# Starting with half the queries, spreading the first keys, values and weight pieces, and moving the last gates to VectorE, in a top-k attention and two-MLP kernel

## The chip, the core and the metric

The kernel runs on one NeuronCore of a Trainium2 chip. The core has five engines with a program each, which run in their own order and wait for one another through semaphores: TensorE (PE in the rows; PEld is its weight load), VectorE (DVE), ScalarE (ACT), GpSimd (POOL) and SyncE (SP). SP issues every transfer of this kernel. The metric is the device time of one execution in microseconds (us); lower is better.

## The reference

Four batches of eight heads with 576 positions and 64 dimensions each go through an attention that keeps the 32 largest scores of each row, then through two MLPs on 2304 rows of 512 values, with 2048 hidden units and no normalisation between them.

```
scores = (q @ k^T) / 8                        # q, k, v: (4, 8, 576, 64)
kth    = 32nd largest of each row of scores
scores = where(scores >= kth, scores, -1e9)
attn   = softmax(scores);  x = attn @ v       # x: (2304, 512)
h = x @ w_in1;  x = (h * sigmoid(h)) @ w_out1 # w_in1: (512, 2048), w_out1: (2048, 512)
h = x @ w_in2;  out = elu(h) @ w_out2
```

## The kernel before

**Tiles and slots.** The 2304 rows are cut into 18 chunks of 128 rows, and a chunk has one tile per head, 144 tiles in all. The program is one loop over slots, `for s in ...: slot(s)`. In slot s, DVE does the first half of tile s's top-k and the second half of tile s-1's. A top-k is four MAX8 (eight largest, L622), three MATCH_REPLACE8 (strike them out, L626) and one masked product (L645) on 128x576 values. PE makes tile s+1's scores S (L587) and multiplies tile s-3's weights with the values (L690).

**MLP steps.** From slot 12 on most slots also hold one MLP step, four steps for a chunk and layer, 12 slots between the layers. A step's 48 matmuls h (L750) stand in slot s, its gate in s+1, its 12 matmuls a (L798) in s+2. The gate is: ACT reads h from PSUM and makes u and t (`emit_act`, L764 to L772), POOL combines them into t (`emit_g`, L778), ACT rounds t to float16 (`emit_ghi`, L782) and POOL forms the remainder (`emit_glo`, L162). The tile of u has one buffer, those of t, gh and the h banks two each. After the last tile's slot only MLP steps are left, and the last four steps, of chunk 17 in layer two, stand in slots 160 to 163.

**Between the layers.** When a chunk's first MLP is complete, `x2_copy` reads it (L811), a sum of squares gives a power-of-two scale, and ACT scales and rounds it (`x_hi`, L159 and L719); POOL forms the remainder (`x_lo`, L162) and SP issues the transposing transfer xt<-x (`x_tp`, L729) that layer two's h needs. In before this stands at the end of the slot five after the step (`p5`).

**Weights.** The four weight matrices arrive as 64-bit numbers, in 64 pieces of 512 KB (`w_load`, L258). DVE, ACT and POOL turn them into 32-bit numbers during slots -2 to 11. `PIECES` says how many pieces each of these slots takes. A piece of the first matrix costs one DVE instruction (L283), which needs one from ACT first (y, L276); a piece of the others costs two on DVE (L316, L321). Per pair of pieces there is a POOL addition (L288 or L308). Each matrix then gets a trace (L341, L346) that sets its scale, after which its pieces are rounded at points of three per slot (`w_point`, L365 to L370) or by `w_scaled` and `w_split`.

**Order.** Each engine runs its instructions in the order in which slot() writes them, and `prep(slots, ...)` puts a load, its sum of squares and its rounding into three slots. `late` lists run at a slot's end, and their second halves (`after`) early in the next slot. Every transfer from SP waits for the one eight places before it.

Of the kernel before, what the change touches and what calls it, by code (L numbers as in the profile page):

```python
# [32 lines left out]
def kernel(  # L33
# [493 lines left out]
    def q_hi(ch):  # L527
        t, m = qnat[ch], qsc[ch]
        if ch == 0:
            scaled(t, m[:, 1:2])  # L530
            a = [p.tile([128, H, 2, D], F16, tag=n, name="q16") for p, n in ((x16_p, "x16"), (u_p, "u"))]
            tb = t[:, :, None, :].to_broadcast([128, H, 2, D])
            nc.scalar.activation(out=a[0], in_=tb, func=AF.Copy)
            qnat[ch] = (tb, a)
            return
# [28 lines left out]
    def q_tp(g):  # L564
# [193 lines left out]

    def emit_act(l, ch, i):
        ps = hps.pop((l, ch, i))  # L760
        u = u_p.tile([128, 512], F32, tag="u", name="u")
        t = t_p.tile([128, 512], F32, tag="t", name="t")
        if l == 0:
            nc.scalar.activation(out=u, in_=ps, func=AF.Tanh, scale=c1[ch])  # L764
            nc.scalar.activation(out=t, in_=ps, func=AF.Copy)
            nc.scalar.activation(out=u, in_=u, func=AF.Identity, scale=G1, bias=g1)
        else:
            c = c2[ch]
            nc.scalar.activation(out=u, in_=ps, func=AF.Relu, scale=c[:, 1:2])
# [443 lines left out]
```

## Time and profile before

| | before |
|---|---|
| median of 3 runs | 1114.62 us (1113.91 to 1117.53) |
| the profiled execution | 1119.21 us, of it 1117.5 us span |
| PE busy | 995.0 us (89%) |
| DVE busy | 941.4 us (84%) |
| ACT busy | 884.2 us (79%) |
| POOL busy | 811.8 us (73%) |
| tile 0's first MAX8 starts | 17.02 us |
| tile 12's first MAX8 starts | 177.33 us |
| tile 143's masked product ends | 1018.00 us |
| last matmul ends | 1113.75 us |

The span runs from the first to the last instruction of the profiled execution. An engine's busy share is a mean over three quite different stages: the start to about 180 us, in which the weights are converted, the middle, and the end from 1018 us on, in which DVE has nearly nothing left.

### The profile page before, as it was taken

The page shows a single profiled execution, that of the slowest core. Times are in us where ns is not written, and L with a number is a line of the kernel's source. Part 1 is how long each engine was busy: PE and PEld are TensorE (multiplying, and loading weights), DVE is VectorE, ACT ScalarE, POOL GpSimd, SP SyncE. Part 2 cuts the span into 40 slices and gives each one's busy share as a digit, 9 for nine tenths or more (in the row PEclk, how much of TensorE's full clock was granted, in tenths as well). Part 3 has the DMA queues.
Part 4 walks back from the last instruction along what each step waited for, and adds up shares of the span by engine and source line. Part 5 has one row for each costly group of instructions (what it writes and reads, how often), then busy time and mean ns, then how long its engine had stood idle before and what let it go on. Part 6 is the DMA issues. An engine that isn't in the chain of part 4 may idle for free.

```text
span 1117.5 us, 30872 instructions
## 1 busy us (share of the span) xinstructions
PE 995.0 (89%) x11956; PEld 715.7 (64%) x11956; DVE 941.4 (84%) x2203; ACT 884.2 (79%) x1539; POOL 811.8 (73%) x971
## 2 busy tenths in 40 slices
PE   1265778689999999999999999999999999999997
PEld 0223336366766777777767777776677777777755
DVE  2899998999898999999998999999899999994000
ACT  6877767989887898989888898988777777776554
POOL 4787886877777777777777777877767676776643
PEclk9978889889999999999999999999999999999999
DMA  7999883555587656566676756567755545443100
GB/s 263 323 270 276 249 205 86 101 94 115 114 136 141 119 95 121 117 110 123 122 160 144 120 111 114 118 114 132 135 101 105 92 83 82 87 68 54 30 20 10
DMA packets 386034, 141.34 MB, mean 126 GB/s; under 512 B 361568, under 2 KB 368736, under 8 KB 385888
## 3 DMA queue, kind: packets, MB, share of 16 engines
q1 hardware_dynamic: 385888, 139.38, 60.6%
q8 instruction: 93, 1.52, 0.6%
q14 instruction: 53, 0.43, 0.1%
HBM read 52.17 MB, written 21.10 MB: 66 GB/s over the span
## 4 chain that ended last, share of the span: by engine, by line
PE 36%; POOL 20%; issue 10%; DVE 8%; DMA 5%; ACT 4%; SPq 0%; POOLq 0%; ACTq 0%; DVEq 0%
PE h L750 16%; PE a L798 15%; POOL t L778 5%; POOL gh L162 4%; DVE r L626 3%; DVE m L622 3%; POOL e L671 3%; DMA xt<-x 2%; PE S L587 2%; PE av L690 2%; POOL W L671 2%; DMA et<-e 2%; POOL x L162 1%; DVE e L645 1%; ACT gh L782 1%
## 5 line engine op out<-in xcount | busy, mean ns | idle before, releaser
L750 PE MATMUL h<-xt,W 128*128 128x128 f16 x6912 | 413.2, 220 | 9.2 <-DMA xt<-x 8.3
L750 PEld LDWEIGHTS <-W 128*128 128x128 f16 x6912 | 397.5, 98 | 22.9 <-DMA xt<-x 10.1
L798 PE MATMUL a<-W,gh 128*128 128x512 f16 x1728 | 397.4, 379 | 4.1 <-POOL gh L162 2.0
L622 DVE MAX8 m<-r 128x8 f32<-128x576 f32 x432 | 313.0, 750 | 2.6
L798 PEld LDWEIGHTS <-gh 128*128 128x128 f16 x1728 | 159.1, 98 | 178.1 <-POOL gh L162 5.0
L162 POOL TENSOR_TENSOR gh<-t,gh 128x512 f16<-128x512 f32 x144 | 167.1, 1160 | 69.8 <-ACT gh L782 69.8
L626 DVE MATCH_REPLACE8 r<-m,r 128x576 f32<-128x576 f32 x288 | 214.2, 744 | 0.0
L778 POOL TENSOR_TENSOR t<-u,t 128x512 f32<-128x512 f32 x144 | 183.2, 1272 | 29.9 <-ACT u L772 23.5
L782 ACT ACTIVATE gh<-t 128x512 f16<-128x512 f32 x144 | 90.2, 627 | 90.5 <-POOL t L778 89.3
L637 ACT ACTIVATE e<-S,bias,c 128x576 f32<-128x576 f32 x144 | 119.8, 832 | 43.2 <-DVE r L626 23.9
L671 POOL TENSOR_TENSOR e<-e,e 128x512 f16<-128x512 f32 x87 | 100.9, 1160 | 71.7 <-ACT e L665 69.5
L587 PE MATMUL S<-kt,qt 128*128 128x288 f16 (+1 forms) x640 | 97.4, 293 | 48.7 <-DVE sv L134 19.5
L622 DVE MAX8 m<-S 128x8 f32<-128x576 f32 x144 | 109.6, 761 | 32.7 <-PE S L587 32.4
L587 PEld LDWEIGHTS <-qt 128*128 128x128 f16 (+1 forms) x640 | 55.3, 101 | 105.4 <-issue 49.2
L645 DVE SCALAR_TENSOR_TENSOR e<-S,m,e 128x576 f32<-128x576 f32 x144 | 115.5, 802 | 0.1
L626 DVE MATCH_REPLACE8 r<-m,S 128x576 f32<-128x576 f32 x144 | 107.7, 748 | 0.0
L671 POOL TENSOR_TENSOR W<-e,W 128x512 f16<-128x512 f32 x57 | 66.2, 1161 | 44.7 <-ACT W L665 38.7
L690 PE MATMUL av<-vt,et 128*128 128x64 f16 (+1 forms) x2100 | 79.9, 195 | 9.0 <-DMA et<-e 8.8
L690 PEld LDWEIGHTS <-et 128*128 128x128 f16 (+1 forms) x2240 | 73.7, 101 | 17.2 <-DMA et<-e 10.8
L665 ACT ACTIVATE e<-e 128x576 f16<-128x576 f32 x87 | 58.8, 676 | 24.9 <-DVE e L645 9.5
L365 PE MATMUL lo<-W,eye 128*128 128x512 f32 x84 | 54.9, 741 | 20.6 <-ACT W L370 12.7
L635 ACT ACTIVATE bias<-m,fixed,c 128x1 f32<-128x1 f32 x144 | 54.1, 376 | 9.6 <-DVE m L622 9.4
(128 smaller groups left out, 1272.5 us busy)
## 6 DMA issues: line engine op xcount, KB each, us to landing
W<-in_moe_w_in_dram SPq DMA_DIRECT2D x32, 512.0 KB, 7.4
W<-in_moe_w_out_dram SPq DMA_DIRECT2D x20, 512.0 KB, 5.8
qd<-q SPq DMA_DIRECT2D x34, 256.0 KB, 5.0
kn<-in_k_dram SPq DMA_DIRECT2D x16, 288.0 KB, 3.2
qn<-in_q_dram SPq DMA_DIRECT2D x16, 256.0 KB, 3.4
out_dram<-o SPq DMA_DIRECT2D x16, 256.0 KB, 2.5
vd<-v SPq DMA_DIRECT2D x12, 320.0 KB, 2.7
vt<-vd SPq DMA_DIRECT2D x22, 160.0 KB, 2.9
```

Of the source, the lines that this page charges most:

```text
L162: nc.gpsimd.tensor_tensor(dst, x, hi, op=ALU.subtract)
L587: nc.tensor.matmul(out=ps[n * e:n * e + n, a, 0:HALF], lhsT=qt[:, 2 * (t % 2) + p, n * e:n * e + n], rhs=kT[bh][:, a * HALF:(a + 1) * HALF ...
L622: nc.vector.max(st["m8"][:, i, :], src if i == 0 else st["r"])
L626: nc.vector.match_replace(out=fold(r) if i == 0 else r, in_to_replace=st["m8"][:, i, :], in_values=src if i == 0 else r, imm_value=LOW,)
L637: nc.scalar.activation(out=fold(e), in_=src, func=AF.Exp, scale=c[:, 0:1], bias=bias)
L645: nc.vector.scalar_tensor_tensor(e, src, st["m8"][:, n - 1, 7:8], e, op0=ALU.is_ge, op1=ALU.mult, accum_out=sums[ch][:, j:j + 1])
L671: nc.gpsimd.tensor_tensor(h[:, S + LO:2 * S], e[:, 0:SF], h[:, 0:SF], op=ALU.subtract)
L690: nc.tensor.matmul(out=avs[ch][n * e:n * e + n, bh[1], :], lhsT=et[:, c, n * e:n * e + n], rhs=vT[bh][:, x, y:y + D], start=(i == 0), stop ...
L750: nc.tensor.matmul(out=ps[:, f:f + 128], lhsT=w, rhs=xt[:, z, :], start=(kk == 0 and x == 0), stop=(kk == KDM - 1 and x == 2),)
L778: nc.gpsimd.tensor_tensor(t, u, t, op=ALU.add if l else ALU.mult)
L782: nc.scalar.activation(out=gh[:, 0, :], in_=gf[l, ch, i], func=AF.Copy)
L798: nc.tensor.matmul(out=acc, lhsT=gh[:, z, u * 128:(u + 1) * 128], rhs=W[:, n, w * 512:(w + 1) * 512], start=(m == 0 and x == 0), stop=(m = ...
```

## The change

The change has three parts.

**The start.** Chunk 0's queries are rounded in two halves of four heads (`q_first_hi`, `q_first_lo`). Half 0 is done first, before the keys; half 1 at the end of slot 0. One transfer per pair of heads takes high and low parts together, where there were two. Three weight pieces are loaded ahead of the second keys instead of five. `PIECES` takes two pieces off slot -1 and four off slot 0, and gives six to each of slots 1 to 7. `KEYS0` and `VALUES0` place the first batch's keys and values by hand. In slots 0 to 2 the weight loads stand behind the transposing transfers.

**Conversion.** One more pair of the third matrix goes by `w_scaled` in slot 11 rather than by a point, three pieces of the fourth change order, and its scale is made one slot later (`traced`).

**The end.** From slot 149 (`ALONE`) on a gate is three DVE instructions in place of two on POOL and one on ACT. The last step's gate and ACT part are cut into halves of 256 columns (`parts`), and the last output leaves in two halves, one by ACT and one by DVE. Chunk 17's x_hi, x_lo and x_tp move from the end of slot 156 into the middle of slot 155 (`p4`).

```diff
         if ch == 0:
             scaled(t, m[:, 1:2])
-            a = [p.tile([128, H, 2, D], F16, tag=n, name="q16") for p, n in ((x16_p, "x16"), (u_p, "u"))]
...
-            nc.scalar.activation(out=a[0], in_=tb, func=AF.Copy)
...
+            a = [p.tile([128, H // 2, 2, 2, D], F16, tag=n, name="q16") for p, n in ((x16_p, "x16"), (u_p, "u"))]
...
+            q_first_hi(0)
             return
...
+    def q_first_hi(x):
+        t, a = qnat[0][x]
+        nc.scalar.activation(out=a[:, :, 0], in_=t, func=AF.Copy)
+
+    def q_first_lo(x):
+        t, a = qnat[0][x]
+        sub(a[:, :, 1], t, a[:, :, 0])
+        if x == 0:
+            q_tp(0)
...
+    def parts(l, ch, i):
+        n = 2 if (l, ch, i) == (1, NCH - 1, NS - 1) else 1
+        return [slice(512 // n * x, 512 // n * (x + 1)) for x in range(n)]
...
     def emit_g(l, ch, i):
+        op = ALU.add if l else ALU.mult
+        if slot_now[0] >= ALONE:
...
+            for z in parts(l, ch, i):
+                nc.vector.tensor_tensor(t[:, z], u[:, z], t[:, z], op=op)
+                nc.vector.tensor_scalar(gh[:, 0, z], t[:, z], 1.0, None, op0=ALU.mult)
+                nc.vector.tensor_tensor(gh[:, 1, z], t[:, z], gh[:, 0, z], op=ALU.subtract)
+            return
...
+            for y in (0, 256):
+                if y:
+                    nc.vector.tensor_scalar(o[:, y:y + 256], acc[:, y:y + 256], t[:, 4:5], None, op0=ALU.mult)
+                else:
+                    nc.scalar.activation(out=o[:, y:y + 256], in_=acc[:, y:y + 256], func=AF.Copy, scale=t[:, 4:5])
+                nc.sync.dma_start(out=out[r0:r0 + 128, y:y + 256], in_=o[:, y:y + 256])
...
+    ALONE = NTILE + 5
...
-    PIECES = (2, 2, 6, 6, 4, 6, 4, 6, 4, 6, 5, 5, 4, 4)
+    PIECES = (2, 0, 2, 6, 6, 6, 6, 6, 6, 6, 5, 5, 4, 4)
...
+    KEYS0 = ((-5, -4, -3), (-4, -2, -1), (0, 1, 1), (1, 3, 3))
+    VALUES0 = ((0, 2, 2), (1, 3, 3), (3, 4, 5), (5, 6, 7))
...
-        wload[(-5, -5, -5, -4, -4, -2, -2, -2, -1, -1, -1, -1, -1, -1, -1, -1)[n]].append((0, n, None))
+        wload[(-5, -5, -5, -2, -2, -2, -2, -1, -1, -1, -1, -1, -1, -1, -1, -1)[n]].append((0, n, None))
...
-        early[slot_now[0]].append(lambda: w_ops(j, m))
+        early[slot_now[0] + (j == 3)].append(lambda: w_ops(j, m))
...
-        for x in wload[s - 1]:
-            w_load(*x)
+        if not 0 <= s < 3:
+            for x in wload[s - 1]:
+                w_load(*x)
...
         while after:
             after.pop(0)()
+        if 0 <= s < 3:
+            for x in wload[s - 1]:
+                w_load(*x)
...
+        if p4 and p4 == (0, NCH - 1, NS - 1):
+            while small_ops:
+                small_ops.pop(0)()
+            x_hi(1, p4[1])
+            x_lo(1, p4[1])
+            x_tp(1, p4[1])
...
-        if p5 and p5 == (0, p5[1], NS - 1):
+        if p5 and p5 == (0, p5[1], NS - 1) and p5[1] < NCH - 1:
```

The first place is SP's program at the start. Before (qn, kn, vn are loads of queries, keys and values, W of weight pieces, qt and kt the transposing transfers):

```order
L412 DMA qn<-in_q_dram 128x8x64
L394 DMA kn<-in_k_dram 128x576
L258 DMA W<-in_moe_w_in_dram 128x1024 x5
L394 DMA kn<-in_k_dram 128x576
L570 DMA_TRANSPOSE qt<-q_186 128x2x128
L570 DMA_TRANSPOSE qt<-q_187 128x2x128
L454 DMA_TRANSPOSE kt<-k_181 128x9x64 x2
L400 DMA vn<-in_v_dram 64x2x256
L401 DMA vn<-in_v_dram 64x2x64
L402 DMA vn<-in_v_dram 64x2x320
L394 DMA kn<-in_k_dram 128x576
L258 DMA W<-in_moe_w_in_dram 128x1024 x11
```

The same place of the changed kernel:

```order
L412 DMA qn<-in_q_dram 128x8x64
L394 DMA kn<-in_k_dram 128x576
L258 DMA W<-in_moe_w_in_dram 128x1024 x3
L394 DMA kn<-in_k_dram 128x576
L581 DMA_TRANSPOSE qt<-q_173 128x4x128
L454 DMA_TRANSPOSE kt<-k_188 128x9x64 x2
L258 DMA W<-in_moe_w_in_dram 128x1024 x4
L400 DMA vn<-in_v_dram 64x2x256
L401 DMA vn<-in_v_dram 64x2x64
L402 DMA vn<-in_v_dram 64x2x320
L394 DMA kn<-in_k_dram 128x576
L454 DMA_TRANSPOSE kt<-k_227 128x9x64 x2
```

Three pieces instead of five stand ahead of the second keys, one query transfer instead of two ahead of the first kt, and the second keys' kt stand ahead of the last nine pieces.

The second place is DVE's program in slot 0. Before, from tile 0's first MAX (m_271) to tile 1's (m_333); L283 is a weight piece:

```order
L622 MAX m_271<-S 128x8
L626 MATCH_REPLACE r<-m_271,S 128x576
L283 SCALAR_TENSOR_TENSOR W<-W,y 128x512
L622 MAX m_271<-r 128x8
L283 SCALAR_TENSOR_TENSOR W<-W,y 128x512
L626 MATCH_REPLACE r<-m_271,r 128x576
L283 SCALAR_TENSOR_TENSOR W<-W,y 128x512 x4
L622 MAX m_271<-r 128x8
L131 TENSOR_SCALAR p_318<-S 128x1
L131 TENSOR_SCALAR p_319<-S 128x1
L622 MAX m_333<-S 128x8
```

Of the change, again from tile 0's first MAX (m_259) to tile 1's (m_300):

```order
L631 MAX m_259<-S 128x8
L635 MATCH_REPLACE r<-m_259,S 128x576
L631 MAX m_259<-r 128x8
L635 MATCH_REPLACE r<-m_259,r 128x576
L283 SCALAR_TENSOR_TENSOR W<-W,y 128x512 x2
L631 MAX m_259<-r 128x8
L631 MAX m_300<-S 128x8
```

Two L283 in place of six, and they stand behind four instructions of tile 0 instead of between them.

The third place is ACT's program near the end, from the middle of slot 155's step (u<-h for step 3 of chunk 16 in layer two) to the first step of chunk 17. Before:

```order
L769 ACTIVATE u<-h,c_18140 128x512
L770 ACTIVATE t<-h 128x512
L771 ACTIVATE u<-u 128x512
L772 ACTIVATE u<-u,c_18140 128x512
L782 ACTIVATE gh<-t 128x512
L159 ACTIVATE y<-y,z 128x512
L719 ACTIVATE x_18829<-y 128x512
L844 ACTIVATE o<-a,c_18140 128x512
L769 ACTIVATE u<-h,c_18734 128x512
```

Of the change, from the two instructions of x_hi on:

```order
L159 ACTIVATE y<-y,z 128x512
L728 ACTIVATE x_18787<-y 128x512
L784 ACTIVATE u<-h,c_18132 128x512
L785 ACTIVATE t<-h 128x512
L786 ACTIVATE u<-u 128x512
L787 ACTIVATE u<-u,c_18132 128x512
L879 ACTIVATE o<-a,c_18132 128x512
L784 ACTIVATE u<-h,c_18726 128x512
```

The scaling and rounding of chunk 17 (y<-y,z and x<-y) stands ahead of that step's four instructions instead of behind them, and the gh<-t is gone.

## Rows read from the trace of the kernel before

**Rows 1.** Page, busy time (us, share, instructions) and the span in 40 slices.

```profile
PE 995.0 (89%) x11956; PEld 715.7 (64%) x11956; DVE 941.4 (84%) x2203; ACT 884.2 (79%) x1539; POOL 811.8 (73%) x971
...
DVE  2899998999898999999998999999899999994000
```

**Rows 2.** Windows (stretch, length, busy us by engine, clock, DMA), start, middle and end.

```profile
0.00:17.00 17.00, 1.44 (x6) 0.64 (x6) 3.82 (x18) 11.03 (x18) 6.76 (x11) 1.00 0.72 229
17.00:33.00 16.00, 1.47 (x6) 0.69 (x6) 7.69 (x16) 11.34 (x20) 8.68 (x6) 1.00 0.95 345
...
sum 183.00, PE 96.89 PEld 50.56 DVE 151.11 ACT 132.19 POOL 134.60; mean PE 6.92 PEld 3.61 DVE 10.79 ACT 9.44 POOL 9.61
...
600.00:800.00 200.00, 198.02 (x2564) 147.67 (x2562) 189.34 (x446) 169.93 (x308) 151.60 (x195) 1.00 0.65 120
...
1085.00:1095.00 10.00, 7.94 (x105) 7.33 (x103) 0.00 (x0) 3.19 (x5) 0.09 (x1) 0.83 0.21 52
```

**Rows 3.** Waits of DVE, 0 to 183 us (waiter, releaser: total us, times, longest).

```profile
DVE W L283 <- ACT y L276: 11.7, 5, 5.2
DVE p L131 <- PE S L171: 11.5, 4, 4.4
```

**Rows 4.** Timeline, start (start us, us, what, [idle before <-releaser]).

```profile
4.55 1.00 SPq L394 DMA_DIRECT2D kn<-in_k_dram  x1
...
8.40 1.06 ACT L533 ACTIVATE q<-qn 128x1024 f16<-128x1024 f32 x1
...
9.54 2.14 POOL L162 TENSOR_TENSOR q<-qn,q 128x1024 f16<-128x1024 f32 x1 [0.42 <-ACT q L533]
...
12.93 2.59 SPq L454 DMA_TRANSPOSE kt<-k  x2
...
14.13 0.68 ACT L156 ACTIVATE sq<-kn 128x576 fp8e4<-128x576 f32 x1 [2.45 <-DMA kn<-in_k_dram]
...
17.02 0.77 DVE L622 MAX8 m<-S 128x8 f32<-128x576 f32 x1 [0.16 <-PE S L587]
...
23.88 0.69 DVE L283 SCALAR_TENSOR_TENSOR W<-W,y 128x512 int32<-128x512 int32 x1 [5.24 <-ACT y L276]
...
32.96 0.76 DVE L622 MAX8 m<-S 128x8 f32<-128x576 f32 x1
...
189.62 0.16 DVE L131 TENSOR_SCALAR p<-gram 128x1 int32<-128x1 int32 x1 [1.40 <-PE gram L171]
```

**Rows 5.** Chain that ended last, 1040 to 1060 us (start us, us, what).

```profile
1048.40 2.68 PE h L750 x48
1051.08 2.59 PE a L798 x12
```

**Rows 6.** Timeline, end of the span.

```profile
1075.20 0.15 DVE L141 TENSOR_SCALAR z<-z 128x1 int32<-128x1 int32 x1
...
1084.63 1.23 SPq L729 DMA_TRANSPOSE xt<-x  x1
...
1087.78 9.84 PE L750 MATMUL h<-xt,W 128*128 128x128 f16 x144 [2.06 <-DMA xt<-x]
1092.30 0.69 ACT L769 ACTIVATE u<-h,c 128x512 f32<-128x512 f32 x1 [5.85 <-PE h L750]
...
1094.02 0.81 ACT L772 ACTIVATE u<-u,c 128x512 f32<-128x512 f32 x1
...
1111.42 2.33 PE L798 MATMUL a<-W,gh 128*128 128x512 f16 x10 [0.62 <-POOL gh L162]
```

**Rows 7.** Groups by line, 1018 to 1118 us (busy us, mean ns, idle before).

```profile
L778 POOL TENSOR_TENSOR t<-u,t 128x512 f32<-128x512 f32 x17 | 21.5, 1265 | 29.9 <-ACT u L772 23.5 <-ACT u L766 6.4
...
L162 POOL TENSOR_TENSOR gh<-t,gh 128x512 f16<-128x512 f32 x17 | 19.7, 1156 | 11.9 <-ACT gh L782 11.9
...
L811 DVE TENSOR_SCALAR y<-a 128x512 f32<-128x512 f32 x2 | 1.4, 692 | 39.9 <-PE a L798 39.9
...
L709 DVE TENSOR_TENSOR xs<-av,sum 128x512 f32<-128x512 f32 x1 | 0.7, 692 | 1.9 <-PE av L690 1.9
```

More of the change, by code (lines that the diff above doesn't have):

```diff
@@ L773, in emit_act @@
-        us[l, ch, i] = u
-        gf[l, ch, i] = t
-    def emit_g(l, ch, i):
+        u_ = u_p.tile([128, 512], F32, tag="u", name="u")
+        t_ = t_p.tile([128, 512], F32, tag="t", name="t")
+        for z in parts(l, ch, i):
+            u, t, p = u_[:, z], t_[:, z], ps[:, z]
+            if l == 0:
+                nc.scalar.activation(out=u, in_=p, func=AF.Tanh, scale=c1[ch])
+                nc.scalar.activation(out=t, in_=p, func=AF.Copy)
+                nc.scalar.activation(out=u, in_=u, func=AF.Identity, scale=G1, bias=g1)
+            else:
+                c = c2[ch]
+                nc.scalar.activation(out=u, in_=p, func=AF.Relu, scale=c[:, 1:2])
+                nc.scalar.activation(out=t, in_=p, func=AF.Relu, scale=G2)
+                nc.scalar.activation(out=u, in_=u, func=AF.Exp, scale=-1.0)
+                nc.scalar.activation(out=u, in_=u, func=AF.Identity, scale=c[:, 2:3], bias=c[:, 3:4])
@@ new lines, in emit_act @@
+        us[l, ch, i] = u_
+        gf[l, ch, i] = t_
+    def emit_g(l, ch, i):
+        op = ALU.add if l else ALU.mult
+        if slot_now[0] >= ALONE:
+            t, u = gf.pop((l, ch, i)), us.pop((l, ch, i))
+            gh = gh_p.tile([128, 2, 512], F16, tag="gh", name="gh")
+            gs[l, ch, i] = gh
+            for z in parts(l, ch, i):
+                nc.vector.tensor_tensor(t[:, z], u[:, z], t[:, z], op=op)
+                nc.vector.tensor_scalar(gh[:, 0, z], t[:, z], 1.0, None, op0=ALU.mult)
+                nc.vector.tensor_tensor(gh[:, 1, z], t[:, z], gh[:, 0, z], op=ALU.subtract)
+            return
@@ L777, in emit_g @@
         t, u = gf[l, ch, i], us.pop((l, ch, i))
-        nc.gpsimd.tensor_tensor(t, u, t, op=ALU.add if l else ALU.mult)
+        nc.gpsimd.tensor_tensor(t, u, t, op=op)
     def emit_ghi(l, ch, i):
@@ L946 @@
         ends.append(end)
-    pairs = [(j, p) for j in range(3) for p in range(NWP // 2)][:-3]
-    for x, n in ((LAG, NWP - 6), (LAG + 1, NWP - 4), (LAG + 2, NWP - 2)):
+    pairs = [(j, p) for j in range(3) for p in range(NWP // 2)][:-4]
+    for x, n in ((LAG - 1, NWP - 8), (LAG, NWP - 6), (LAG + 1, NWP - 4), (LAG + 2, NWP - 2)):
         late[x].append((partial(w_scaled, 2, n), None))
@@ L969 @@
             jj, nn = freed[j][n]
-            x = max(d - 2, dec[jj].get((nn, None), dec[jj].get((nn, 0))))
+            x = max(d - (3 if j == 1 and n < 8 else 2), dec[jj].get((nn, None), dec[jj].get((nn, 0))))
             for e in es:
@@ L1011, in slot @@
         slot_now[0] = s
-        cur, p1, p2, p5 = (mlp_step(s - x) for x in (0, 1, 2, 5))
+        cur, p1, p2, p4, p5 = (mlp_step(s - x) for x in (0, 1, 2, 4, 5))
         if 0 <= s < NTILE:
@@ L1089, in slot @@
             o[0]()
+        if p4 and p4 == (0, NCH - 1, NS - 1):
[4 more added lines that the diff above has]
+            x_tp(1, p4[1])
+            tiny[s].append(partial(x2_inv_ops, p4[1]))
         dv(a, b, a, more=False)
-        if p1:
+        if p1 and s < ALONE:
             emit_ghi(*p1)
@@ L1139, in slot @@
             ahead.clear()
-        for f in sumsq[s]:
-            f()
+        if not -1 <= s < 8:
+            for f in sumsq[s]:
+                f()
         for hi, lo in late[s]:
@@ L1146, in slot @@
                 after.append(lo)
+        if -1 <= s < 8:
+            for f in sumsq[s]:
+                f()
         while stores:
```

52 lines of the change are left out of this document (22 added, 30 removed).

## The prediction

> **What bounds the kernel now.** I read the busy line of the page and DVE's slices first. PE is busy 995 of 1117.5 us, and DVE is at eight to nine tenths from the second slice to the 36th and then stops [rows 1]. So there are three stages, and each has to be read by itself. The windows say which engine has no slack in each. Up to 183 us DVE is busy 151.1 us and PE only 96.9: DVE bounds the start, and what can be won there is its 31.9 us of idle time. Of that, 13.2 us lie before 17 us and 8.3 us between 17 and 33 us [rows 2]. From 600 to 800 us PE is busy 198.0 of 200 us: PE bounds the middle, and no instruction of the middle is changed [rows 2]. In the tail the chain of waits is h, a, h, a on PE, 2.68 + 2.59 = 5.27 us for a step [rows 5], until the last chunk. An earlier start therefore moves the whole middle forward, because the middle's work is the same and stands in the same order.
>
> The waits of DVE say what the idle time of the start waits for: 11.7 us for ACT's y, the longest 5.2, and 11.5 us for PE's sums [rows 3]. The timeline has the places. DVE's first MAX8 starts at 17.02; then an L283 that stands ahead of tile 0's other work waits 5.24 us, and tile 1's first MAX8 starts only at 32.96 [rows 4]. At the end of the span PE waits 2.06 us for xt<-x of chunk 17, and the 144 matmuls behind that wait take 9.84 us, where three times 2.68 would be 8.0 [rows 5, 6].
>
> **The start, part by part.** *Halved queries.* Before, kt's transfer is issued at 12.93, behind ACT's copy of 1024 columns (1.06 us, ending at 9.46), POOL's remainder of 2.14 us and two query transfers [rows 4]. A 512-column remainder on POOL takes 1.16 [rows 7], and the copy lies between half of 1.06 and the 0.69 of a 512-column ACT instruction [rows 6]. ACT now does queries first and keys second, and is done about 0.4 us sooner, near 9.0; POOL's remainder of the keys takes 1.16 us and a small piece, to about 10.4. So kt is issued about 2.5 us earlier, and S and the first MAX8 follow: 17.02 becomes 14.5. The bounds are 0 (the transfers are no faster for being early) and 3.5.
>
> *Slot -1's two pieces* leave DVE's idle time before 17 us and come back later as work on the bounding engine: two L283 of 0.69 [rows 4], minus 1.4 us.
>
> *Slot 0's pieces.* Two L283 in place of six stand between tile 0's first MAX8 and tile 1's, behind four top-k instructions. The wait of 5.24 us was DVE standing in its own order behind a piece that ACT reached late. With four top-k instructions ahead of it (4 x 0.77 = 3.1 us) and only keys ahead of it on ACT, I take this wait as gone, and the other three of the stretch, 8.3 - 5.2 = 3.1 us, as staying. So 5.2 us, with bounds of 0 and 8.3. The four pieces are not saved but done in slots 2, 4 and 6, where DVE is busy anyway; that costs nothing, since DVE's work is a sum.
>
> *Fewer pieces ahead.* The second keys were issued at 4.55 and ACT could use them only at 14.13, behind five pieces of 512 KB [rows 4]. With three pieces the wait is shorter, which the 5.2 us need. The Trainium skill ("DMA: Bandwidth & Descriptors", Queues, rings and completion order) says that each DMA engine consumes its descriptors in ring order. The trace agrees: 9.6 us from issue to use there, though ACT was ready 2.45 us before. The same rule speaks against the other half of the change: nine pieces now stand behind the second keys' transposing transfers on SP.
>
> *The fourth matrix's scale* is made a slot later: DVE's wait of 1.40 us at 189.62 [rows 4] goes, since the sum is then long there. Bounds 0 and 1.4. The pair done by w_scaled, the changed order of three pieces and the later sums of squares move work among ACT, POOL and PE, which have 50.8, 48.4 and 86.1 us idle up to 183 [rows 2]; I cost them at nothing. Were that cover gone, a pair would cost two ACT passes of 1024 columns, 2 x 1.06 = 2.1 us [rows 4].
>
> Sum of the start: 2.5 - 1.4 + 5.2 + 1.4 = 7.7 us. With the lower bounds it is -1.4, with the upper 11.8.
>
> **The tail.** *x_hi moved up.* The scale z is ready at 1075.35, but x is issued only at 1084.63 and lands at 1087.78, 3.15 us later [rows 6]. In the change DVE first has the three gate instructions of the step before, 3 x 0.69 = 2.1 us, so z comes near 1077.4; two ACT instructions of 0.69 lead to 1078.8, POOL's 1.16 to 1080.0 and the transfer to 1083.1. PE is done with the a matmuls ahead at 1087.78 - 2.06 = 1085.72. So the wait of 2.06 us goes with 2.6 us to spare. Queued behind the two ACT instructions is the ACT part of the last step of chunk 16, 1.3 us later than before; its gate is 1.0 us shorter on DVE, and PE's a for it would wait a few tenths more. I leave this at nothing.
>
> *The clock.* Granted is 0.83 in the window from 1085 to 1095, so 1.7 of its 10 us are lost at the lower of the two levels, 1.2 GHz, right behind the gap [rows 2]. Without the gap I take them back. The Trainium skill ("TensorE: Matmul & The Clock Gate", Part 1) says that the array's clock is halved by default and that activity releases it. By that rule the 1.7 us come back; if the level fell for another reason the sum would be 1.7 smaller. The trace agrees as far as the fall follows the gap.
>
> *Gates on DVE.* The last four steps take from 1087.78 to the end of the last matmul, 1111.42 + 2.33 = 1113.75, so 25.97 us, where four times 5.27 would be 21.1 [rows 5, 6]. Of the 4.9 us above that, 1.7 are the clock and 3.2 are PE waiting for gates. Such a gate took 1.27 on POOL, 0.69 for 512 columns on ACT and 1.16 on POOL, 3.1 us [rows 6, 7]. No row has DVE doing this from SBUF; the nearest are 0.69 for a product and 0.69 for a copy of 512 columns read from PSUM [rows 7], so three take 2.1 us. ACT's part of a step takes 1092.30 to 1094.83, 2.5 us [rows 6], and the next may write u when DVE's first instruction has read it: 2.5 + 0.7 = 3.2 us for a step, under PE's 5.27. PE then never waits, and the 3.2 us go. If a DVE instruction took twice 0.69, the period would be 3.9, still under 5.27. The last step's halves only shorten a gate that PE reaches late anyway: nothing. The output in halves trades 0.3 us of ACT for a second transfer: nothing. Gates in slots 149 to 155 cost nothing, since PE's chain of h and a has no wait for them [rows 5].
>
> Sum of the tail: 2.1 + 1.7 + 3.2 = 7.0 us, between 2.1 (only the gap) and 7.5.
>
> **The sum.** 7.7 + 7.0 = 14.7 us. The profiled execution took 1119.21 us, 1.7 more than its span, so it would take 1104.5. It is 4.6 us above the median of the runs shown; against the median of 1114.62 the forecast is 1099.9 us.
>
> **The rivals.** *The start gives nothing back.* The nine pieces behind keys and queries land later, and slots 1 to 3 with six pieces wait for them where slot 0 waited. For it: SP's program, and DMA at 345 GB/s already between 17 and 33 us [rows 2]. The ring order of the Trainium skill's page on DMA would bring the same about. Against it: the sixteen pieces of the first matrix are now needed by slot 2 rather than slot 1. The start gives 2.5 - 1.4 = 1.1, the tail 7.0, so 1106.5.
>
> *The clock falls again or the gates hold.* Then the tail gives only the gap, 2.1, the start 7.7: 1104.8.
>
> *Slower.* Six pieces in each of slots 2 to 6 make another engine the bound there. POOL has three additions of weights in each, and the remainders of weights, keys and values; it is busy 134.6 of 183 us on the whole [rows 2], and weight space is only free for the next load when it has added. If each of these five slots waits more than 14.7 / 5 = 2.9 us, the kernel is slower; at 4 us it takes 1114.62 - 14.7 + 20 = 1119.9. Against it: the pieces up to slot 6 are 40 in both kernels, so POOL gets no more work.
>
> *It doesn't show.* The middle might not follow the start, if its slots hang on something that keeps its time. No row speaks for that; with the tail's bound of 2.1 it would be 1112.5.
>
> **How the numbers follow.** Forecast 0.62, the start giving nothing 0.20, the tail giving only the gap 0.06, no effect 0.05, slower 0.07. About 0.3%, 3.3 us, is what a measurement of this kernel can tell from no change: faster 0.88, same 0.05, slower 0.07. The likeliest case's own range is 1095 to 1104. The range of 1094 to 1108 takes in the first three cases and most of the bounds of both sums.
>
> **What would show it.** Right: the first MAX8 near 14.5 and tile 1's near 20; tile 12's near 170 (177.33 before); no PE wait for the last xt<-x; the last four steps in about 21 us at a clock of 1.0; the last matmul 14 to 15 us earlier. The start is wrong if DVE waits for ACT's y or for weight transfers in slots 1 to 3 by as much as it did in slot 0; the tail is wrong if PE shows idle time before a with gh from DVE, or a clock below 1 behind 1085. The whole is wrong if tile 12 is early and tile 143 isn't.

## The result, and the profile after

| | before | changed |
|---|---|---|
| median | 1114.26 us (4 runs, 1113.80 to 1117.53) | 1103.43 us (4 runs, 1102.56 to 1105.52) |
| ratio | | 0.990, 95% interval 0.9881 to 0.9919 |
| the profiled execution | 1119.21 us | 1103.00 us |
| tile 0's first MAX8 | 17.02 us | 14.06 us |
| tile 12's first MAX8 | 177.33 us | 169.61 us |
| tile 143's masked product ends | 1018.00 us | 1007.85 us |
| last matmul ends | 1113.75 us | 1097.19 us |

The change makes the kernel 10.8 us faster; the forecast was 14.7, and 1099.9 us in all. The profiled executions differ by 16.2 us, which is more than the medians do: before's lies 5.0 us above the median of this table, the changed kernel's 0.4 below its own. So a difference of these two traces must not be read as the worth of the change.

The page of the changed kernel, busy times and DVE's slices, answers to [rows 1]:

```profile
PE 987.7 (90%) x11950; PEld 713.3 (65%) x11950; DVE 967.0 (88%) x2243; ACT 875.3 (79%) x1530; POOL 786.3 (71%) x950
...
DVE  4999999999898999999999999999999999996232
```

DVE is at eight or nine tenths from the second slice to the 36th, and now has work until the last one: those are the gates.

The windows of the changed kernel (stretch, length, busy time by engine, clock, DMA share, GB/s) answer to [rows 2]:

```profile
0.00:17.00 17.00, 2.59 (x10) 1.08 (x10) 5.93 (x22) 11.00 (x20) 7.20 (x13) 1.00 0.70 227
17.00:33.00 16.00, 1.12 (x5) 0.57 (x5) 11.37 (x24) 12.02 (x19) 8.68 (x6) 1.00 1.05 310
600.00:800.00 200.00, 198.83 (x2562) 146.82 (x2561) 190.49 (x448) 171.16 (x310) 153.49 (x196) 1.00 0.63 121
```

By 33 us DVE has worked 5.93 + 11.37 = 17.3 us where it had worked 3.82 + 7.69 = 11.5, so 5.8 us more, and 4.6 of the second stretch are still idle. The middle is as full of PE as it was.

The start of the changed kernel in the timeline, against [rows 4]; the first two rows are SP's queue, the rest DVE:

```profile
10.18 2.53 SPq L454 DMA_TRANSPOSE kt<-k  x2
18.36 3.03 SPq L454 DMA_TRANSPOSE kt<-k  x2
...
6.31 0.16 DVE L131 TENSOR_SCALAR p<-S 128x1 int32<-128x1 int32 x1 [1.39 <-PE S L171]
...
14.06 0.77 DVE L631 MAX8 m<-S 128x8 f32<-128x576 f32 x1 [1.38 <-PE S L596]
...
19.12 0.75 DVE L631 MAX8 m<-S 128x8 f32<-128x576 f32 x1
...
26.47 0.69 DVE L283 SCALAR_TENSOR_TENSOR W<-W,y 128x512 int32<-128x512 int32 x1 [2.43 <-ACT y L276]
...
181.90 0.16 DVE L131 TENSOR_SCALAR p<-gram 128x1 int32<-128x1 int32 x1 [0.61 <-PE gram L171]
```

The first kt is issued 2.75 us earlier and the first MAX8 starts 2.96 earlier; tile 1's starts at 19.12 instead of 32.96. But a wait for ACT's y is back in slot 1, 2.43 us long. The row at 6.31 is DVE's first work on the first keys' sum, which needs their load; it is used below.

The end of the changed kernel, against [rows 6]: PE's last groups, then one gate on DVE and the ACT instruction that waits for it, then the output's halves.

```profile
1067.77 8.35 PE L823 MATMUL a<-W,gh 128*128 128x512 f16 x36
1075.95 8.20 PE L759 MATMUL h<-xt,W 128*128 128x128 f16 x144
1083.99 2.75 PE L823 MATMUL a<-W,gh 128*128 128x512 f16 x12
1086.58 2.84 PE L759 MATMUL h<-xt,W 128*128 128x128 f16 x48
1089.26 7.93 PE L823 MATMUL a<-W,gh 128*128 128x512 f16 x36
...
1084.81 0.69 DVE L798 TENSOR_TENSOR t<-u,t 128x512 f32<-128x512 f32 x1 [1.41 <-ACT u L787]
1085.61 0.43 DVE L799 TENSOR_SCALAR gh<-t 128x512 f16<-128x512 f32 x1
1086.07 0.69 DVE L800 TENSOR_TENSOR gh<-t,gh 128x512 f16<-128x512 f32 x1
...
1085.60 0.69 ACT L784 ACTIVATE u<-h,c 128x512 f32<-128x512 f32 x1 [0.82 <-DVE t L798]
...
1097.29 0.47 ACT L876 ACTIVATE o<-a,c 128x256 f32<-128x256 f32 x1 [4.58 <-PE a L823]
...
1097.80 0.48 DVE L874 TENSOR_SCALAR o<-a,c 128x256 f32<-128x256 f32 x1 [3.84 <-ACT o L876]
```

PE has no wait among these groups; the 144 matmuls take 8.20 us instead of 9.84, and the last four steps 21.2 us instead of 25.97. The gate is 0.69 + 0.43 + 0.69 us of work. DVE's half of the output starts only when ACT's half is done.

### The profile page after: what moved, and what is told of

It reads as the page before. It is cut to its first block, busy times and chain, and to the rows that moved or that the text cites. A ratio compares the mean times of both kernels' runs of the same rounds, so it can differ in the third digit from the quotient of the medians.

```text
span 1101.3 us, 30867 instructions
## 1 busy us (share of the span) xinstructions
PE 987.7 (90%) x11950; PEld 713.3 (65%) x11950; DVE 967.0 (88%) x2243; ACT 875.3 (79%) x1530; POOL 786.3 (71%) x950
## 4 chain that ended last, share of the span: by engine, by line
PE 34%; POOL 23%; issue 10%; ACT 7%; DVE 5%; DMA 5%; POOLq 0%; ACTq 0%; DVEq 0%; SPq 0%
PE h L759 15%; PE a L823 14%; POOL t L803 5%; POOL gh L162 5%; POOL e L680 4%; POOL W L680 3%; PE S L596 2%; PE av L699 2%; DMA xt<-x 2%; DVE r L635 2%; DVE m L631 2%; POOL x L162 1%; ACT gh L807 1%; DMA kd<-k 1%; POOL W L162 1%
## 5 line engine op out<-in xcount | busy, mean ns | idle before, releaser
L162 POOL TENSOR_TENSOR gh<-t,gh 128x512 f16<-128x512 f32 x132 | 153.2, 1161 | 59.7 <-ACT gh L807 59.7
L803 POOL TENSOR_TENSOR t<-u,t 128x512 f32<-128x512 f32 x132 | 168.0, 1272 | 1.0 <-ACT u L787 1.0
L807 ACT ACTIVATE gh<-t 128x512 f16<-128x512 f32 x132 | 82.8, 627 | 80.8 <-POOL t L803 79.8
L699 PEld LDWEIGHTS <-et 128*128 128x128 f16 (+1 forms) x2240 | 73.3, 101 | 19.9 <-DMA et<-e 12.1
L365 PE MATMUL lo<-W,eye 128*128 128x512 f32 x80 | 50.4, 716 | 16.1 <-ACT W L370 14.3
L787 ACT ACTIVATE u<-u,c 128x512 f32<-128x512 f32 (+1 forms) x73 | 59.0, 808 | 2.4
```

The costliest lines, as they stand in the source:

```text
L162: nc.gpsimd.tensor_tensor(dst, x, hi, op=ALU.subtract)
L699: nc.tensor.matmul(out=avs[ch][n * e:n * e + n, bh[1], :], lhsT=et[:, c, n * e:n * e + n], rhs=vT[bh][:, x, y:y + D], start=(i == 0), stop ...
L803: nc.gpsimd.tensor_tensor(t, u, t, op=op)
L807: nc.scalar.activation(out=gh[:, 0, :], in_=gf[l, ch, i], func=AF.Copy)
```

## The experiments

Each kernel is before or the changed kernel with the edit shown. Ratios are to before on the same chip, with a 95% interval. A ratio is taken from all runs, so what it gives in us can differ a little from the difference of two medians.

### Which part gives what: the end and the start apart, and the end's two halves

The end alone (e1_tail) is before with `parts`, `ALONE`, `p4` and the output in halves. The start alone (e2_start) is the changed kernel without them. Two more take the end apart: e3_xhi adds the first two hunks below to before; e4_gates adds the last one, with `parts` and the three DVE instructions of `emit_g`. The output in halves is in neither.

```diff
+        if p4 and p4 == (0, NCH - 1, NS - 1):
+            while small_ops:
+                small_ops.pop(0)()
+            x_hi(1, p4[1])
+            x_lo(1, p4[1])
+            x_tp(1, p4[1])
+            tiny[s].append(partial(x2_inv_ops, p4[1]))
...
-        if p5 and p5 == (0, p5[1], NS - 1):
+        if p5 and p5 == (0, p5[1], NS - 1) and p5[1] < NCH - 1:
...
-        if p1:
+        if p1 and s < ALONE:
             emit_ghi(*p1)
             emit_glo(*p1)
```

Expected of e1_tail: 

> Before, with the three edits of the end alone: chunk 17's rounding moved up, gates on VectorE from slot 149, the last output in halves. Theory A (the two profiles can be trusted): the end gives 6.1 us against before, because the last matmul came 6.4 us earlier relative to tile 143 and the output lost 0.35; ratio 0.9945. Theory B (the profiled execution of before was 4.6 us above its median, and part of the end's gain, the 1.7 us of a lower clock and some of the gap, is only in that execution): 3 to 4.4 us, ratio 0.996 to 0.997. As predicted: 7.0 us, 0.9937.

Expected of e2_start: 

> The changed kernel with the end as before, so that only the edits up to 180 us stand (queries in halves, PIECES, KEYS0 and VALUES0, loads, w_scaled pair, later scale). Theory A: 7.0 us against before by the first MAX8 of tiles 19 to 61 in the two profiles, ratio 0.9937, and then the two parts together would be 13 and not the 10.8 measured. Theory B (the end is the smaller one): 7.0, and the end alone 3.8. Theory C (the start is the smaller one, the middle gives some back in ordinary executions): 4.7, ratio 0.9958, and the end alone 6.1.

Expected of e3_xhi: 

> Before, with chunk 17's rounding and transfer moved up to slot 155 and nothing else; the gates stay on POOL and ACT. As predicted the gap of 2.06 us ahead of chunk 17's h goes, and the clock of 0.83 behind it, if the gap is its cause: 2.1 + 1.7 = 3.8 us faster, clock 1.0 from 1085 to 1095. If the clock has another cause: 2.1. Rival: the gates of the last four steps are reached that much earlier and hold PE longer, since ACT and POOL get the early rounding into their queues ahead of a gate: 0 to 1 us.

Expected of e4_gates: 

> Before, with the gates from slot 149 on VectorE and the last gate and ACT part in halves; chunk 17's rounding stays where it was, at the end of slot 156. As predicted PE's waits of 3.2 us for gates in the last four steps go: 3.2 us faster, and the gap of 2.06 us ahead of chunk 17's h is still there or up to 1 us longer, since z stands behind a gate on VectorE. Rival: the gates are hidden anyway, PE's idle time there is the pipeline filling after the gap: 0 to 1 us.

| | median | ratio | faster by (interval of the ratio) |
|---|---|---|---|
| before, in this group | 1114.67 us | | |
| e1_tail, the end alone | 1109.39 us | 0.9951 (0.9933 to 0.9968) | 5.3 us (3.6 to 7.5) |
| e2_start, the start alone | 1108.92 us | 0.9947 (0.9932 to 0.9962) | 5.8 us (4.2 to 7.6) |
| e3_xhi, rounding moved up alone | 1112.64 us | 0.9982 (0.9969 to 0.9994) | 2.0 us (0.7 to 3.5) |
| e4_gates, gates on DVE alone | 1108.98 us | 0.9947 (0.9933 to 0.9962) | 5.7 us (4.2 to 7.5) |

The two parts add up: 5.3 + 5.8 = 11.1, against 10.8 measured together. By the medians both parts are smaller than the two profiles had made them, but the intervals exclude none of the theories; the traces have to decide, and more than one execution of them. From the end of tile 143's masked product to the last matmul, the start alone, with the old end, takes 94.50 us, the changed kernel 89.34: 5.2, less 0.3 us that the changed kernel needs longer from the last matmul to the end, so 4.9. Before's own profile takes 95.76 there, since its 144 matmuls take 9.84 us where e2's take 8.21. For the start, tile 19's first MAX8 comes at 218.91 to 221.24 in the four profiles with the old start (before, e1, e3, e4), 219.94 on average; in the changed kernel, its repetition below and e2 at 213.87 to 214.38, average 214.10: 5.8. Before's own profile is the latest of its four, by 1.3 us against their average.

PE's timeline of e2_start, which has the old end, shows what is new there:

```profile
1078.50 8.21 PE L759 MATMUL h<-xt,W 128*128 128x128 f16 x144 [2.00 <-DMA xt<-x]
```

and a window of it inside those 144 matmuls:

```profile
1081.60:1086.60 5.00, 5.00 (x93) 5.00 (x91) 0.00 (x0) 3.58 (x7) 1.85 (x2) 1.00 0.01 3
```

The same gap of 2.0 us is there, and the clock does not fall behind it: 8.21 us, clock 1.00, which is the upper level, 2.4 GHz. Another kernel with the old end (p1_pieces, below) has the fall, in PE's timeline:

```profile
1089.77 9.84 PE L750 MATMUL h<-xt,W 128*128 128x128 f16 x144 [2.07 <-DMA xt<-x]
```

and in the window:

```profile
1090.00:1095.00 5.00, 5.00 (x65) 5.00 (x62) 0.00 (x0) 0.71 (x2) 0.00 (x0) 0.66 0.01 5
```

The 0.66 is a mean over time at both levels. So with this gap of 2 us the lower level, 1.2 GHz, follows in two executions of three (before's, this one; not e2's). In e4_gates the gap is half as long (PE's timeline):

```profile
1083.58 8.20 PE L750 MATMUL h<-xt,W 128*128 128x128 f16 x144 [1.06 <-DMA xt<-x]
```

There it does not fall, nor in any of the ten profiles without the gap. The Trainium skill ("TensorE: Matmul & The Clock Gate", Part 1) says that activity releases the clock; that a pause of one and the same length costs the clock in one execution and not in another, these traces show beside it.

From the start of the 144 h to the last matmul, e2 takes 24.35 us and e4 21.24: the gates on DVE are worth 3.1 us there. They shorten the gap by 0.94 as well, though the rounding stayed where it was, where the expectation had it stay or grow. That is why e4 gives more than the 3.2 us expected, and why moving the rounding up is worth 2.0 alone and less on top of the gates: from the end of the masked product to the last matmul e2 takes 94.50, e4 89.62, and e1, which has both, 88.72. In e3_xhi the 2.0 us is what the gap alone was expected to give; the 3.8 of gap and clock together lie outside its interval.

### Which edit of the start does it

Each undoes one of them in the changed kernel. s1_whole rounds all queries before the first transfer:

```diff
             q_first_hi(0)
+            q_first_hi(1)
             return
...
             q_first_lo(0)
+            q_first_lo(1)
             return
...
-    late[0].append((partial(q_first_hi, 1), partial(q_first_lo, 1)))
```

s2_pieces has before's PIECES, s4_scale before's slot for the fourth scale, and s3_loads before's list of the first matrix's loads and before's place for those of slots 0 to 2 (that the second matrix's first eight pieces are loaded a slot earlier stays):

```diff
-    PIECES = (2, 0, 2, 6, 6, 6, 6, 6, 6, 6, 5, 5, 4, 4)
+    PIECES = (2, 2, 6, 6, 4, 6, 4, 6, 4, 6, 5, 5, 4, 4)
...
-        early[slot_now[0] + (j == 3)].append(lambda: w_ops(j, m))
+        early[slot_now[0]].append(lambda: w_ops(j, m))
...
-        if not 0 <= s < 3:
-            for x in wload[s - 1]:
-                w_load(*x)
+        for x in wload[s - 1]:
+            w_load(*x)
...
-        wload[(-5, -5, -5, -2, -2, -2, -2, -1, -1, -1, -1, -1, -1, -1, -1, -1)[n]].append((0, n, None))
+        wload[(-5, -5, -5, -4, -4, -2, -2, -2, -1, -1, -1, -1, -1, -1, -1, -1)[n]].append((0, n, None))
```

Expected of s1_whole: 

> The changed kernel with chunk 0's queries rounded whole again, though still ahead of the keys: both halves' copies follow each other on ACT and both remainders on POOL before the first transfers. All else as changed. Theory A (the halving is what brings the first MAX8 forward, as in the sum): the copy costs ACT about 0.5 us more and POOL's remainders 1.16 more ahead of the keys' remainder, so tile 0's first MAX8 comes at 15.5 to 16.5 in place of 14.06, and the kernel loses 1.5 to 2.5 us of the 10.8. Theory B (the first MAX8 hangs on the transfers, or slot 1 waits for weight pieces anyway): tile 0 moves by under 0.5 us or the delay is gone by tile 4, and the kernel loses nothing.

Expected of s2_pieces: 

> The changed kernel with PIECES of before: two pieces in slot -1 and six in slot 0, four in slots 2, 4 and 6. The halved queries, the early transposes and the loads stay as changed. Theory A (the piece spreading took the 5.24 us wait out of slot 0, as in the sum): 5.2 - 1.4 = 3.8 us are lost, 7 us faster than before, and DVE waits 4 to 6 us for ACT's y between tile 0's and tile 1's first MAX8. Theory B (the wait went because the keys and queries come earlier): at most 1 us lost, and slot 0's wait stays under 2 us.

Expected of s3_loads: 

> The changed kernel with the weight loads as before: five pieces ahead of the second keys' use rather than three, and the later loads of slots 0 to 2 ahead of the transposing transfers. Theory A (the order of the loads is needed for the gain of the start): the second keys reach ACT 2 to 4 us later, ACT's y and the pieces of slots 0 and 1 follow, and 2 to 5 us are lost. Theory B (ring order hurts in the changed kernel: the nine pieces stand behind the second kt, and DVE waits 2.43 us at 24.04 for a piece that lands late): that wait goes and up to 2.4 us are gained. In between: nothing, since both happen.

Expected of s4_scale: 

> The changed kernel with the fourth matrix's scale made in the slot of its trace, as before, instead of a slot later. Theory A (the sum's term of 1.4 us): DVE waits 1.4 us or more for PE's gram at about 182, tile 14 and all that follows come 1.0 to 1.4 us later, and 1.0 to 1.4 us are lost. Theory B (another wait ends at the same place, as 0.61 us of wait for the gram stayed in the changed kernel): 0.8 us or less is lost, too little to tell in the time, and only the wait shows it.

| | median | ratio | faster by, from the ratio |
|---|---|---|---|
| before, in this group | 1113.99 us | | |
| s1_whole | 1103.90 us | 0.990 (0.988 to 0.9921) | 11.1 us |
| s2_pieces | 1111.99 us | 0.9979 (0.9965 to 0.9992) | 2.3 us |
| s3_loads | 1108.28 us | 0.9936 (0.9912 to 0.9961) | 7.1 us |
| s4_scale | 1101.62 us | 0.9891 (0.9869 to 0.9912) | 12.1 us |

The changed kernel's ratio of 0.990 would be 11.1 us here.

**Halving is worth 0.9 us at kt, and nothing that the time shows.** In s1_whole's timeline (DVE and SP's queue) kt is issued at the same time as in the changed kernel and the first MAX8 starts as early:

```profile
5.46 0.16 DVE L131 TENSOR_SCALAR p<-S 128x1 int32<-128x1 int32 x1 [0.52 <-PE S L171]
...
10.24 2.53 SPq L454 DMA_TRANSPOSE kt<-k  x2
...
14.13 0.77 DVE L633 MAX8 m<-S 128x8 f32<-128x576 f32 x1 [1.79 <-PE S L598]
```

Yet the first row, DVE's start on the first keys' sum, is at 5.46 here and at 6.31 in the changed kernel: in that execution the first keys came 0.85 us later. Counted from this row, kt is issued 4.78 us later in s1_whole and 3.87 in the changed kernel, as in all seven other profiles with halved queries; the first MAX8 follows after 8.67 in s1_whole and 7.75 in the changed kernel. So halving brings both forward by 0.9 us in this count, less than theory A's 1.4 to 2.4; theory B holds for the time, in which no loss is seen. In before the same distance to kt is 12.93 - 5.39 = 7.54 us. The other 2.8 of the 3.7 us come with the queries' place ahead of the keys and the one transfer for high and low parts, which are not separated further. Before's rows, the first keys' sum on DVE and POOL's remainder of the keys, show what they act on:

```profile
5.39 0.16 DVE L131 TENSOR_SCALAR p<-S 128x1 int32<-128x1 int32 x1 [4.42 <-PE S L171]
...
7.70 1.42 POOL L162 TENSOR_TENSOR k<-kn,k 128x512 f16<-128x512 f32 x2 [6.35 <-ACT k L435]
```

The keys are ready for kt at 9.12 there, but kt stands in SP's queue behind the queries' two transfers, whose remainder POOL ends at 11.68.

**PIECES undone costs more than the start is worth:** 11.1 - 2.3 = 8.8 us against 5.8, where theory A had 3.8. DVE's timeline in s2_pieces, then two rows of ACT:

```profile
16.28 0.69 DVE L283 SCALAR_TENSOR_TENSOR W<-W,y 128x512 int32<-128x512 int32 x1 [3.30 <-ACT y L276]
...
16.95 0.76 DVE L631 MAX8 m<-S 128x8 f32<-128x576 f32 x1
...
29.61 0.69 DVE L283 SCALAR_TENSOR_TENSOR W<-W,y 128x512 int32<-128x512 int32 x1 [5.82 <-ACT y L276]
...
15.62 0.62 ACT L276 ACTIVATE y<-W 128x512 int32<-128x512 uint16 x1 [3.43 <-DMA W<-in_moe_w_in_dram]
...
28.96 0.62 ACT L276 ACTIVATE y<-W 128x512 int32<-128x512 uint16 x1 [5.88 <-DMA W<-in_moe_w_in_dram]
```

The first MAX8 is back near 17, though kt is issued at 9.38 there: the two pieces of slot -1 stand ahead of it on DVE and wait 3.30 us for ACT. And slot 0's long wait is back, as theory A had it, 5.82 us. But in both places ACT itself waits for a weight transfer, since three pieces are loaded ahead of the transposes and before's PIECES needs more by then. In before ACT came late to slot 0's piece for another reason, the values that stand ahead of it:

```profile
20.18 0.74 ACT L156 ACTIVATE sq<-vn 128x640 fp8e4<-128x640 f32 x1 [3.05 <-DMA vn<-in_v_dram]
```

So s2_pieces shows that the old PIECES and the new loads do not go together, and not what PIECES is worth by itself. That the start without it would be slower than before's is not shown: tile 19's first MAX8 is at 221.08, within the 218.91 to 221.24 of the old start.

**The loads' order:** DVE and PE in the timeline of s3_loads:

```profile
15.48 0.77 DVE L631 MAX8 m<-S 128x8 f32<-128x576 f32 x1 [3.17 <-PE S L596]
...
34.08 0.16 DVE L131 TENSOR_SCALAR p<-S 128x1 int32<-128x1 int32 x1 [4.98 <-PE S L171]
...
32.87 1.14 PE L596 MATMUL S<-kt,qt 128*128 128x288 f16 x4 [16.46 <-DMA qt<-q]
```

Both theories' effects are there. The waits for y in slot 1, 4.5 us in the changed kernel, are gone, but the first MAX8 is 1.4 us later, and with eight loads ahead the second kt is issued at 22.15 instead of 18.36 and the qt behind it at 27.91 instead of 21.96. PE's scores wait for that qt until 32.87, the matmul for the next keys' scale (L171) stands behind them on PE, and DVE waits 4.98 us for it. By the times the one costs more than the other gives back, 11.1 - 7.1 = 4.0 us, though the two intervals overlap.

What the waits for y in the changed kernel hang on, its ACT rows show:

```profile
25.15 0.68 ACT L156 ACTIVATE sq<-kn 128x576 fp8e4<-128x576 f32 x1 [0.83 <-DMA kn<-in_k_dram]
...
25.83 0.61 ACT L276 ACTIVATE y<-W 128x512 int32<-128x512 uint16 x1
...
28.24 0.62 ACT L276 ACTIVATE y<-W 128x512 int32<-128x512 uint16 x1 [0.63 <-DMA W<-in_moe_w_in_dram]
```

The y at 25.83, for which DVE waits 2.43 us, needs none of the nine loads: it stands on ACT behind half 1's rounding and the third keys, which land only at 25.15. The y at 28.24, for which DVE waits 1.06, does wait for the first of the nine.

**The later scale is worth nothing.** In s4_scale the wait is 1.40 us again, as theory A had it, yet the time is no worse. The changed kernel has three waits of DVE behind it that s4_scale does not have up to 216 us (at 188.06 for S, 0.24 us, and these):

```profile
194.23 0.77 DVE L631 MAX8 m<-S 128x8 f32<-128x576 f32 x1 [0.37 <-PE S L596]
...
209.63 0.20 DVE L1155 RECIPROCAL sum<-sum 128x8 f32<-128x8 f32 x1 [0.90 <-POOL sum L146]
```

The two waits for S, 0.61 us together, are in all six profiles with the later scale and in none with the early one, so of the 0.8 us that the wait for the gram shrinks by, 0.2 are left. The third, of 0.7 to 1.6 us, does not belong to the edit: three of the eight profiles with the early scale have one too. Over all profiles, tiles 13 to 19 take 38.8 to 39.7 us with the later scale (six profiles) and 38.2 (five) or 39.6 to 39.9 (three) with the early one. In time the two cannot be told apart.

### PIECES alone, and two attempts at more

p1_pieces is before with the changed PIECES and nothing else. c1_better is the changed kernel with the early scale and the output whole; c2_split adds to it that two of the nine loads go ahead of the second kt; a_again is the changed kernel once more.

```diff
-        if not 0 <= s < 3:
-            for x in wload[s - 1]:
-                w_load(*x)
+        n = 0 if 1 <= s < 3 else 2 if s == 0 else 99
+        for x in wload[s - 1][:n]:
+            w_load(*x)
...
-        if 0 <= s < 3:
-            for x in wload[s - 1]:
-                w_load(*x)
+        for x in wload[s - 1][n:]:
+            w_load(*x)
```

Expected of p1_pieces: 

> Before, with the changed PIECES alone: slot -1 empty, two pieces in slot 0, six in slots 1 to 7. Queries, keys, values, loads, scale and the end stay as before. Theory A (the spreading of pieces is nearly all of the start, and halved queries are worth nothing of their own): tile 0's first MAX8 near 14.5 to 15.5, no L283 wait over 2.5 us in slot 0, 4 to 6 us faster than before. Theory B (the edits of the start only work together, as the changed kernel with PIECES of before lost 8.5 us): slots 1 and 2 wait for keys or weight pieces instead, and the kernel is 0 to 2 us faster or slower.

Expected of c1_better: 

> The changed kernel with two of its edits undone: the fourth matrix's scale again in the slot of its trace, and the last output whole from ACT in one transfer. From the traces: the later scale takes 0.8 us from the wait for the gram but tile 19 comes 0.9 us later relative to tile 13, so undoing it gives 0.5 to 1.8 us; the halves cost 0.15 to 0.35 us behind the last matmul. Theory A: 0.7 to 2 us faster than the changed kernel on the same chip. Theory B (both are within what can't be told): equal within 0.7 us.

Expected of c2_split: 

> As the run before it (early scale, whole output), and two of the nine weight loads that stand behind the second kt and qt are put ahead of them. Theory A (the slow stretch of DMA from 22 to 26 us, 150 GB/s with nothing but transposes issued, is what makes the pieces of slot 1 late): the waits of L283 for ACT's y in slot 1, 4.5 us together in the changed kernel, shrink to 1 to 3, and 1 to 2.5 us are gained. Theory B (ring order): the second kt lands 1.5 to 3 us later, PE's S and with it p wait as they did with all loads ahead (4.98 us), and 0 to 2 us are lost.

Expected of a_again: 

> The changed kernel again, on the chip and beside the runs of before that the other three of this group share, to compare them with. 10 to 12 us faster than before. Its first MAX8 was at 14.06 in the first profile; 13.5 was seen with the same start: 13.5 to 14.1, and tile 12 between 168.5 and 170.

| | median | ratio |
|---|---|---|
| before, in this group | 1115.02 us | |
| p1_pieces | 1120.14 us | 1.0045 (1.0026 to 1.0064) |
| c1_better | 1101.94 us | 0.9876 (0.9849 to 0.9903) |
| c2_split | 1103.31 us | 0.9899 (0.9878 to 0.9920) |
| a_again | 1103.94 us | 0.9898 (0.9879 to 0.9918) |

p1_pieces is 5.1 us slower than before, more than theory B allowed. SP's queue and DVE in its timeline:

```profile
13.24 2.59 SPq L454 DMA_TRANSPOSE kt<-k  x2
...
30.42 4.51 SPq L454 DMA_TRANSPOSE kt<-k  x2
...
17.19 0.77 DVE L622 MAX8 m<-S 128x8 f32<-128x576 f32 x1 [2.27 <-PE S L587]
...
40.02 0.77 DVE L622 MAX8 m<-S 128x8 f32<-128x576 f32 x1 [3.51 <-PE S L587]
```

Without the pieces ahead of it the first MAX8 waits for kt, which is issued as late as in before; the second kt, behind eleven loads, is late for tile 2. Behind that, DVE waits another 2.02 us for y in slot 2. So in before the first MAX8 is held by two chains. DVE's rows of before have the other one:

```profile
15.16 0.16 DVE L131 TENSOR_SCALAR p<-S 128x1 int32<-128x1 int32 x1 [3.87 <-PE S L171]
...
16.11 0.68 DVE L283 SCALAR_TENSOR_TENSOR W<-W,y 128x512 int32<-128x512 int32 x1
```

DVE waits until 15.16 for the second keys' sum, then does the two pieces and is free at 16.86; S follows 0.16 us later. An earlier kt alone could have won 0.16 us, and taking the pieces away alone won next to nothing (17.19). In the changed kernel all three come earlier, the second keys' sum at 11.96, and the first MAX8 starts at 14.06.

c1_better is 2.0 us under the repetition of the changed kernel by the medians, but their intervals overlap: that it is better than the changed kernel is not shown, nor does s4_scale, measured in another group, settle it. It beats before as the changed kernel does. c2_split shows no gain over c1_better: the wait for y behind the nine loads shrinks from 1.06 us to 0.33, but the longest, which hangs on the third keys, is still 2.2.

## Why the prediction came out as it did

The direction and the range held; the size was 3.9 us too large.

- **The start, 7.7 predicted, 5.8 measured (4.2 to 7.6).** *Halved queries, 2.5:* right in size for kt, which is issued at 10.18 where the step said about 10.4. But the step took kt as all that held the first MAX8. The second keys' sum and the two pieces of slot -1 held DVE until 0.16 us before S came, so the gain of 3.0 us needed the other edits too, and of kt's advance the halving itself is 0.9.
- *Slot 0's pieces, 5.2:* the wait went, and so did the other idle time that the step left standing. (The sign "tile 1 near 20" does not fit the step: with 3.1 us of idle time left standing it would be about 22.5.) Tile 1 comes 13.3 us earlier on average of the profiles above, of which six pieces not yet done are 6 x 0.69 = 4.1, so 9.2 are won. But 3.0 are lost again by tile 2 (10.4 earlier, 4.1 of it the pieces) in slot 1's waits for y. The first rival's mechanism, the nine loads, is 1 us of these waits; the longest hangs on the third keys and ACT's order, which no step and no rival had.
- *The fourth scale, 1.4:* mis-sized. The wait shrank by 0.8 only, and 0.6 of that is given back at the next two tiles. Without this term the sum was 6.3, and 6.4 were measured up to tile 13 (181.33 to 174.90 on average). That agreement is luck: at tile 8, where both kernels have done the same 46 pieces, 4.9 are won, and no term of the sum stands for the 1.5 that come between tiles 8 and 13.
- **The end, 7.0 predicted, 4.9 by the traces, 5.3 by the medians (3.6 to 7.5).** *The gap, 2.1:* right in size, 2.0 alone. *Gates, 3.2:* right, 3.1. They overlap, because the gates shorten the gap by half; together they still take out all of both.
- *The clock, 1.7:* the failed step of the end. It was read from one execution as a price that each pays. With the gap it is there in two profiles of three, both of them executions above their medians. There it costs 1.6 us (25.97 against e2's 24.35 from the start of the 144 h to the last matmul), so the size was right and its being in the median wrong. e3_xhi, which takes the gap away, gains 2.0 and not 3.8, so a median holds at most a part of it; how large a part, three executions cannot say.
- *Output in halves, 0:* 0.3 us lost from the last matmul to the end. The halves lie in one accumulator and are read one after the other. The Trainium skill ("PSUM — Partial Sum Buffer", PSUM bank collisions raise a hardware error) says that two engines must not read the same bank at once, in disjoint columns neither. The row with DVE behind ACT's o agrees in that DVE waited; that the bank is the reason no run here shows.
- *DVE's gate, 2.1:* 1.95 from first start to last end. The conversion takes 0.43, not 0.69. The Trainium skill ("VectorE: DVE Perf Modes", the perf-mode tier table) gives a one-input 32-bit instruction from SBUF twice the rate of one with two inputs; 0.43 beside 0.69 agrees in direction (the output here is float16).
- *Signs:* the first MAX8 (14.5 said, 14.06), tile 1 (20, 19.12), tile 12 (170, 169.61), no wait for the last xt and 21.2 us for the last four steps came as said. The last matmul came 16.6 us earlier where 14 to 15 was said, because these are two single executions. Most signs were met although reasons behind them were wrong; only the kernels with one edit undone showed that.
- *Slower:* this rival named POOL. p1_pieces shows that PIECES can indeed cost 5 us, and its first long waits are not for POOL: 3.51 us for S at tile 2, behind transposes that stand late in SP's queue, and 2.02 for y in slot 2, with the order of the start as it was.

What stays open: what the queries' place and the one transfer are worth apart, what the placing of the first keys and values gives by itself (no run undoes it), and whether c1_better's two microseconds are real. Open too is tile 8 to tile 13: it takes 58.4 to 58.9 us in the changed kernel, its repetition and e2, 59.6 to 60.7 in the four profiles with the old start, but 59.9 to 61.1 in s1, s3, s4 and c2, whose start is new. Where it is short, DVE's wait for POOL's addition in slot 11 is 1.3 to 1.6 us, and 2.7 in the others; what sets it was not found.

## What to carry to other kernels

Where two chains end within a fraction of a microsecond of each other ahead of the same instruction, neither edit is worth much alone and the pair is worth all of it; look for the second chain before pricing the first. When a time is compared across two traces, count it from the event that releases it: a first load that lands 0.85 us earlier hid what halving gave. A loss of clock in one profiled execution that lies above its median may belong to that execution alone; price it from a second one. When loads and transposes share one issuing queue, respreading the work that the loads feed pays only if the loads are respread too.

## What the runs showed of the hardware

From 22 to 26 us in the changed kernel the two second kt transfers (issued from 18.36) and the queries' transfer behind them (issued at 21.96) are under way, and DMA moves less than half of what it moves afterwards, at a full busy share. Its windows:

```profile
22.00:26.00 4.00, 0.00 (x0) 0.00 (x0) 1.36 (x2) 3.11 (x6) 1.61 (x2) 1.00 1.18 150
26.00:33.00 7.00, 1.12 (x5) 0.57 (x5) 5.10 (x12) 6.12 (x9) 4.54 (x3) 1.00 1.05 407
```

That is 150 against 407 GB/s (last column), and with eight loads ahead the same two kt transfers take 5.71 us to issue in s3_loads instead of 3.03. That the transposes are the cause is not shown; no run leaves them out. The clock after a pause of 2.0 us differs from execution to execution, as shown above. Between two executions of the same kernel, the middle from tile 19 to tile 143 differs by up to 3 us (785.1 in the changed kernel, 788.0 in its repetition), which bounds what two single traces can tell.
